# Diagonal score groups of two neighbouring steps in one visit, in a gated attention and maxout kernel

## The chip, the cores and the metric

The kernel runs on one core of one Trainium2 chip, as one program. The metric is the device time of that program in microseconds (us). The time before is the median of three runs; one further execution was recorded by the hardware profiler, and its trace is what the readings below come from.

## The reference

```python
# u, v: (8, 3072, 256)   z: (8, 3072, 64)   moe_w1, moe_w2: (256, 1024)   moe_w_out: (1024, 256)
scores = (1 / S) * z @ z.T                 # per batch, 3072 x 3072, symmetric
attn   = maximum(scores, 0) ** 2
x      = u * (attn @ v)                    # reshaped to 24576 x 256
out    = maximum(x @ w1, x @ w2) @ w_out   # float32
```

`attn` is symmetric: the block (i, j) is the transposed block (j, i).

## The kernel before, in words

A batch has 24 blocks of 128 rows, in six groups of four (`G = 4`). One **step** `n = 6b + s` gives the output rows of group `s` of batch `b`, so there are 48 steps. Its score groups are: the *early* ones (g < s), which an earlier step computed and a DMA transpose turned into a tile `aT`; its *own* ones (g > s), which are computed here; and the diagonal one (g = s). Steps are called s0 to s5 below, by their place in the batch. In batch 0 the steps s0 to s2 take a simpler way and have no diagonal group of this kind (`NDIAG = 2`).

**Scores.** A score tile is a pair of PSUM banks, 128 x 2 x 512 float32 (`psum_pair`, the `mm` pool, three tiles in a ring). An own group takes two tiles (`add_pair`): two matmuls of 512 columns each, which contract over 64 rows and run side by side in the two halves of the array. The diagonal group (`add_diag`) takes one full tile, `(n, None)`, for its upper two row blocks, and one tile half used, `(n, -1)`, for the lower right quarter: two matmuls of 256 columns. Its lower left quarter comes from two small DMA transposes, `("turn", n, None, r)`. ScalarE (ACT) or VectorE (DVE) then reads the PSUM tile with `relu` (L219, L221) into `a_sb` (pool A, 12 tiles in a ring), and `square` works in place (L225, L227). Own groups are turned into `aT` by SyncE's DMA queue (SP), four row blocks in two halves: the first half after its square, the second half after the sum `S1` of the step itself.

**A step on TensorE (PE).** Every product of `attn @ v` goes by a seven-product scheme on sums: three products per job in a first pass (`X` jobs, operands as they are) and four in a second pass (`Y` jobs, on sums `S1` to `S4` that DVE puts into `es`, a ring of four tiles, and `a_sb` or `aT`). A step runs on PE in this order: the last layer `o` of the step three before (40 matmuls), the 12 `X` jobs (six groups, two each), the middle layer `d` of the step two before (16 matmuls into four PSUM tiles of the same `mm` ring, each read by a `g` relu), and the 12 `Y` jobs. The groups come in the order `st.groups`: early, own, diagonal. Both passes use the same two accumulators; between the passes, `e0`, `w` and `t` read them while `d` runs, and after `Y` others do while the next step's `o` runs.

**Visits.** Score matmuls are put between the products in runs of up to three tiles (`WIN = 3`), the *windows* of the code; a run is called a visit here. The list of windows is filled in the order of the steps and of their rows (L972 to L978), so that a batch of 42 tiles has 14 visits. Then they are placed from the last to the first (L1015 to L1020): each goes to the last place that begins no later than its due time and at least `GAP` = 2.4 us before the next visit. Due times (`rows_read`) are 6.5 us before the first `X` job that reads an own row, and 11.5 us for turned rows and for the diagonal. A place must lie at least 0.86 us behind the end of `o` or `d` and 1.7 us ahead of the next one (`free`, L990). In a step of 16.97 us by this plan (4.36 `o`, 3.92 `X`, 3.46 `d`, 5.23 `Y`) that leaves the 4th to 7th `X` jobs, and the `Y` jobs from the third to the ninth. With 2.4 us between visits, a step has at most three: one in `X`, one ahead of the third `Y` job ("early") and one ahead of the ninth ("late").

**The other queues.** PE's order is written out from this plan. A list scheduler then gives every other piece of work an engine and an order: of the work that could begin first, the one with the earliest due time. Each engine, and SP's DMA queue, works in that order and waits in it. `make_zT`'s two transposes (job `zT`) bring the next batch's `z`; from batch 1 on they are let go 12 us into s3. `uT` turns the step's `u`.

Of the kernel before, what the change touches and what calls it, by code (L numbers as in the profile page):

```python
# [11 lines left out]
def kernel(  # L12
# [27 lines left out]
    P = 128  # L40
    NSB = S // P
    G = 4
    WIN = 3
    GW = G * P
    HW = GW // 2
    NG = NSB // G
# [4 lines left out]
    NDIAG = 2  # L51
# [27 lines left out]
    def matmul(*args, **kw):  # L79
        newest[0] = pin(nc.tensor.matmul(*args, **kw)).ins  # L80
# [57 lines left out]
    def direct(b, i, j):  # L138
        return b == 0 and i < j <= NDIR

    q = seqs[0]
# [19 lines left out]
    class Job:  # L161
        def __init__(self, key, ways, fn, deps, new, uses, after, lag):
            self.key, self.ways, self.fn, self.lag = key, ways, fn, lag
            self.deps, self.new, self.uses, self.after = list(deps), new, list(uses), list(after)
            self.succ, self.waits = [], 0
            self.begin = self.done = None
            self.due = 1e12
# [7 lines left out]
    def job(key, ways, fn, deps=(), new=None, uses=(), after=(), lag=100):  # L175
        assert key not in jobs, key
        jobs[key] = Job(key, ways, fn, deps, new, uses, after, lag)

    def buf(pool, key, make):
        bufs[pool, key] = Buf(make)  # L180
        order.setdefault(pool, []).append(key)

    def tile_of(pool, key):
        return bufs[pool, key].tile

    class Step:
        def __init__(self, n, b, s):
            self.n, self.b, self.s, self.q = n, b, s, seqs[b]
            self.plain = n < PLAIN
            self.count = [0] * KD  # L190
            self.last_plain = [None] * KD
            self.diag = not (b == 0 and s <= NDIAG)
            self.rows = ([None] if self.diag else []) + [
                k0
                for k0 in range(0, NSB, 2)
                if k0 // G > s or direct(b, k0 // G, s) or (k0 // G == s and not self.diag)
            ]
            self.early = [i for i in range(s) if not direct(b, i, s)]
            self.own = sorted({k0 // G for k0 in self.rows if k0 is not None})
            self.groups = self.early + self.own + ([s] if self.diag else [])  # L200

    steps = [Step(n, *divmod(n, NG)) for n in range(B * NG)]

    def score(q, out_ps, j, k, s, q0, n):
        half = ds(j * dqk, dqk)
        matmul(
            out_ps,
            q.zT[half, k + 1 - j, :],
            q.zT[half, ds(G * s + 1 - j + q0, n), :],
            start=True,  # L210
            stop=True,
        )

    def turn(out_ap, in_ap):
        sp_dma(out=out_ap, in_=in_ap, transpose=True)

    def relu(eng, out_ap, in_ap):
        if eng == "ACT":
            pin(nc.scalar.activation(out_ap, in_ap, AF.Relu))  # L219
        else:  # L220
            pin(nc.vector.tensor_single_scalar(out=out_ap, in_=in_ap, scalar=0.0, op=ALU.max))  # L221

    def square(eng, ap):
        if eng == "ACT":
            pin(nc.scalar.activation(ap, ap, AF.Square))  # L225
        else:
            pin(nc.vector.tensor_mul(ap, ap, ap))  # L227
# [33 lines left out]
    def a_tile(st, g):  # L261
        return tile_of(*a_key(st.n, g))
# [52 lines left out]
    def s_tile(key):  # L315
        return tile_of("mm", key)
# [61 lines left out]
    def add_diag(st):  # L378
        n, q, g = st.n, st.q, st.s
        k = G * g  # L380
        a = ("A", (n, g))
        buf("A", (n, g), lambda: apool.tile([P, G, GW], bf16, name="a_sb"))

        def low_blocks():
            return a_tile(st, g).rearrange("p r (q x) -> p r q x", x=P)[:, 2:4, 2:4, :]

        def scores(_):
            for j in range(2):
                score(q, s_tile((n, None))[:, j, :], j, k + j, g, 0, G)

        def scores_low(_):
            ps = s_tile((n, -1))
            score(q, ps[:, 0, 2 * P :], 0, k + 2, g, 2, 2)
            score(q, ps[:, 1, : 2 * P], 1, k + 3, g, 2, 2)

        job(("score", n, None), {"PE": 223}, scores, deps=z_deps(st), new=("mm", (n, None)), lag=150)
        job(("score", n, -1), {"PE": 112}, scores_low, deps=z_deps(st), new=("mm", (n, -1)), lag=150)

        def relu_low(eng):
            ps = s_tile((n, -1)).rearrange("p b (q x) -> p (b q) x", x=P)  # L400
            relu(eng, low_blocks(), ps[:, 2:6, :].rearrange("p (r q) x -> p r q x", r=2))

        job(
            ("relu", n, None),
            RELU,
            lambda eng: relu(eng, a_tile(st, g)[:, 0:2, :], s_tile((n, None))),
            deps=[("score", n, None)],
            new=a,
            uses=[("mm", (n, None)), a],
            lag=200,  # L410
        )
        job(
            ("relu", n, -1),
            RELU_HALF,
            relu_low,
            deps=[("score", n, -1)],
            uses=[("mm", (n, -1)), a],
            after=[("relu", n, None)],
            lag=200,
        )  # L420
        job(
            ("square", n, None),
            SQUARE,
            lambda eng: square(eng, a_tile(st, g)[:, 0:2, :]),
            deps=[("relu", n, None)],
            uses=[a],
            lag=200,
        )
        job(
            ("square", n, -1),  # L430
            SQUARE_HALF,
            lambda eng: square(eng, low_blocks()),
            deps=[("relu", n, -1)],
            uses=[a],
            lag=200,
        )
        for r in range(2):

            def do_turn(_, r=r):
                aD = a_tile(st, g).rearrange("p r (q x) -> p r q x", x=P)  # L440
                turn(aD[:, 2:4, r, :], aD[:, r, 2:4, :].rearrange("p q x -> p (q x)"))

            job(
                ("turn", n, None, r),
                {"SP": 450},
                do_turn,
                deps=[("square", n, None)],
                uses=[a],
                lag=2600,
            )  # L450
# [517 lines left out]
    tiles = []  # L968
    for n, st in enumerate(steps):
        for k0 in st.rows:  # L970
            tiles += [(n, None), (n, -1)] if k0 is None else [(n, k0)]
    windows, room = [], 0  # L972
    for i, (n, k0) in enumerate(tiles):
        if not room or (k0 is None and room < 2):
            windows.append([])
            room = 2 if n == 0 else WIN
        windows[-1].append((n, k0))
        room = 0 if (n + 1) % NG == 0 and k0 == -1 else room - 1  # L978

    begins, t = [], 0  # L980
    for ns, _, _, _ in work:
# [18 lines left out]
    for n in range(PLAIN, len(steps)):  # L1000
        i = first_of[n]
# [13 lines left out]
    for w in reversed(range(len(windows))):  # L1015
        limit = min([limit] + [due[r] for r in windows[w] if r in due])
        found = [i for i in spots if begins[i] <= limit]
        i = found[-1] if found else 0
# [29 lines left out]
    def z_deps(st):  # L1048
        return [("zT", st.b)] if st.b else []
# [45 lines left out]
    for n in range(len(steps)):  # L1095
        b, s = steps[n].b, steps[n].s
        if n == 0:
            add_u(0, None)
        else:
            pb, ps = divmod(n - 1, NG)  # L1100
# [15 lines left out]
    for tile_sb, source, key, at, new, rows in (  # L1116
# [16 lines left out]
        deps=[("w2",)],  # L1133
        new=W2T,
        uses=[W2, W2T],
        after=at_step(0, 1, 7),
        lag=3500,
# [5 lines left out]
        deps=[("w1",), ("w2",)],  # L1143
        uses=[W2],
# [3 lines left out]
    def w2o_products(_):  # L1148
# [15 lines left out]
        deps=[("w2T",), ("wo",)],  # L1164
        new=[("mm", ("w2o", dc)) for dc in range(KD)],
        uses=[W2T],
        lag=150,
    )
    for dc in range(KD):
# [4 lines left out]
            deps=[("w2o",)],  # L1174
            uses=[("mm", ("w2o", dc))],
            lag=200,
# [3 lines left out]
    for st in steps:  # L1180
        for k0 in st.rows:
            add_diag(st) if k0 is None else add_pair(st, k0)
    for args in plain_todo:
        st, i, ks, dcs = args
# [58 lines left out]
    for pool, keys in order.items():  # L1243
        for i, k in enumerate(keys):
            j = taker.get((pool, k))
# [21 lines left out]
    for key, before in zip(pe_order, [None] + pe_order):  # L1267
        j = jobs[key]
# [7 lines left out]
    while stack:  # L1276
        j = stack.pop()
# [49 lines left out]
    while len(emitted) < len(jobs) - len(HEAD):  # L1327
        best = None
        for e, todo in ready.items():
            if e == "DVE":  # L1330
                todo = [r for r in todo if not left_to_act(r[1], r[0])]
            if not todo:
                continue
            at, _, j = min(
                ((max(t, idle_from[e]), j.due, j) for t, j in todo), key=lambda x: x[:2]
            )
# [3 lines left out]
        at, e, j = best  # L1340
# [93 lines left out]
```

## Time and profile before

| | |
|---|---|
| median of 3 runs | 932.8 us (932.5 to 934.61) |
| profiled execution, its time | 930.27 us |
| its span, first to last instruction | 928.5 us |
| granted TensorE clock | 1.000 |
| PE / DVE / ACT busy | 923.0 / 766.3 / 682.2 us |
| score matmuls, 512 columns | x594, 64x512 |
| score matmuls, 256 columns | x90, 64x256 |

The span is 1.8 us below that execution's own time, and the execution lies 2.5 us below the median. In the views, `L80` is the one line from which every matmul is issued, so PE's work is told apart by its tiles: `s_ps<-zT` are scores, `acc<-es,...`, `acc<-aT,...` and `acc<-a_sb,...` the products of `X` and `Y`, `s_ps<-xT,w_sb` the layer `d`, `s_ps<-w_out_sb,g_sb` the layer `o`. On ACT, `g_sb<-s_ps` reads a tile of `d`, `a_sb<-s_ps` a score tile.

### The profile page before, as it was taken

To read this page: it belongs to the slowest core of one execution; us is meant where nothing else is said; L and a number is where in the kernel's file an instruction comes from. 1 tells how busy PE (TensorE), PEld (TensorE's weight loads), DVE (VectorE), ACT (ScalarE), POOL (GpSimd) and SP (SyncE) were. 2 spreads that over 40 slices of the span, in tenths; PEclk is the share of its full clock that TensorE was granted. 3 is DMA by queue.
4 is the path that set the end of the run, shared out by engine and by line. 5 is a ranking of instruction groups with operands and counts; after the bars stand their busy time and mean duration, and the time that the engine had idled before them with its cause. 6 is when DMAs were issued, how large, how long until landed. Compare 5 with 4: busy or idle time off the path is not lost.

```text
span 928.5 us, 18994 instructions
## 1 busy us (share of the span) xinstructions
PE 923.0 (99%) x7343; PEld 668.2 (72%) x7343; DVE 766.3 (83%) x1915; ACT 682.2 (73%) x825; POOL 58.4 (6%) x115
## 2 busy tenths in 40 slices
PE   9999999999999999999999999999999999999998
PEld 3367777777777777777777776777767776777786
DVE  7958997888978888888888888888898887988761
ACT  8867876778777777776877678776888658875634
POOL 2100100000000000001000010000000000000000
PEclk9999999999999999999999999999999999999999
DMA  9999999987989879998999899988898888986611
GB/s 161 151 183 180 179 186 181 158 156 136 160 172 157 151 137 180 165 152 144 151 188 153 153 146 158 172 150 153 144 166 173 149 149 149 183 154 125 121 46 68
DMA packets 372778, 142.54 MB, mean 154 GB/s; under 512 B 351184, under 2 KB 352848, under 8 KB 372688
## 3 DMA queue, kind: packets, MB, share of 16 engines
q1 hardware_dynamic: 356128, 111.60, 64.6%
q0 software_dynamic: 16560, 29.74, 22.9%
q8 instruction: 57, 0.93, 0.4%
q14 instruction: 33, 0.27, 0.1%
HBM read 59.77 MB, written 25.17 MB: 91 GB/s over the span
## 4 chain that ended last, share of the span: by engine, by line
PE 94%; DVE 3%; DMA 1%; issue 0%; ACT 0%; POOL 0%; POOLq 0%
PE s_ps L80 47%; PE acc L80 47%; DVE es L233 1%; DMA v_sb<-in_v_dram 1%; DVE a_sb L221 1%; DVE lf L236 0%; DMA o_sb<-in_z_dram 0%; DVE a_sb L233 0%; DVE xT L240 0%; DVE e L233 0%; DVE a_sb L227 0%; DVE g_sb L221 0%; DVE e L236 0%; ACT a_sb L225 0%; ACT a_sb L219 0%
## 5 line engine op out<-in xcount | busy, mean ns | idle before, releaser
L80 PEld LDWEIGHTS <-v_sb 128*128 128x128 bf16 x2304 | 223.7, 98 | 79.9 <-issue 37.7
L219 ACT ACTIVATE a_sb<-s_ps 128x1024 bf16<-128x1024 f32 (+1 forms) x231 | 211.6, 971 | 30.7 <-PE s_ps L80 28.0
L225 ACT ACTIVATE a_sb<-a_sb 128x1024 bf16<-128x1024 bf16 (+1 forms) x220 | 214.2, 1010 | 0.3
L80 PE MATMUL acc<-es,v_sb 128*128 128x256 bf16 x864 | 197.4, 274 | 0.1
L80 PE MATMUL s_ps<-w_out_sb,g_sb 128*128 128x256 bf16 x1504 | 195.0, 273 | 0.0
L219 ACT ACTIVATE g_sb<-s_ps 128x1024 bf16<-128x1024 f32 x181 | 170.9, 1029 | 13.4 <-PE s_ps L80 13.4
L233 DVE TENSOR_TENSOR es<-a_sb 128x512 bf16<-128x512 bf16 x306 | 121.1, 416 | 66.9 <-PE acc L80 66.9
L80 PEld LDWEIGHTS <-lf 128*128 128x128 bf16 x1620 | 158.3, 98 | 22.6 <-issue 0.3
L80 PE MATMUL s_ps<-xT,w_sb 128*128 128x512 bf16 x768 | 173.6, 379 | 0.0
L80 PE MATMUL acc<-es,lf 128*128 128x256 bf16 x756 | 170.8, 273 | 0.0
L80 PE MATMUL acc<-a_sb,lf 128*128 128x256 bf16 x612 | 166.9, 273 | 0.0
L80 PEld LDWEIGHTS <-g_sb 128*128 128x128 bf16 x1504 | 146.9, 98 | 17.5
L80 PE MATMUL acc<-aT,v_sb 128*128 128x256 bf16 x684 | 143.0, 273 | 0.0
L80 PE MATMUL acc<-a_sb,v_sb 128*128 128x256 bf16 (+1 forms) x740 | 138.9, 291 | 0.3 <-ACT a_sb L225 0.3
L80 PEld LDWEIGHTS <-w_sb 128*128 128x128 bf16 x768 | 75.0, 98 | 81.1 <-issue 0.3
L230 ACT COPY e<-acc 128x512 f32<-128x512 f32 x90 | 53.2, 591 | 108.9 <-PE acc L80 108.5
L221 DVE TENSOR_SCALAR a_sb<-s_ps 128x1024 bf16<-128x1024 f32 (+1 forms) x107 | 121.2, 1133 | 5.1 <-PE s_ps L80 4.8
L230 ACT COPY o_sb<-s_ps 128x512 f32<-128x512 f32 (+1 forms) x92 | 53.1, 577 | 86.3 <-PE s_ps L80 86.3
L80 PE MATMUL s_ps<-zT 64*128 64x512 bf16 (+1 forms) x684 | 92.9, 366 | 0.4 <-DVE zT L110 0.4
L227 DVE TENSOR_TENSOR a_sb<-a_sb 128x1024 bf16<-128x1024 bf16 (+1 forms) x118 | 75.0, 647 | 0.2 <-ACT a_sb L219 0.2
L80 PE MATMUL s_ps<-W2o_sb,xT 128*128 128x256 bf16 x384 | 73.4, 273 | 0.0
L80 PE MATMUL acc<-aT,lf 128*128 128x256 bf16 x252 | 68.7, 273 | 0.0
(60 smaller groups left out, 711.8 us busy)
## 6 DMA issues: line engine op xcount, KB each, us to landing
out_dram<-o_sb SPq DMA_DIRECT2D x47, 512.0 KB, 3.7
v_sb<-in_v_dram POOLq DMA_DIRECT2D x48, 256.0 KB, 5.3
u_sb<-in_u_dram POOLq DMA_DIRECT2D x48, 256.0 KB, 5.3
aT<-a_sb SPq DMA_TRANSPOSE x230, 4.2
z_sb<-in_z_dram POOLq DMA_DIRECT2D x7, 384.0 KB, 5.4
a_sb<-a_sb SPq DMA_TRANSPOSE x90, 3.2
w_sb<-in_moe_w_dram POOLq DMA_DIRECT2D x2, 512.0 KB, 9.6
uT<-u_sb SPq DMA_TRANSPOSE x48, 4.6
```

Of the source, the lines that this page charges most:

```text
L80: newest[0] = pin(nc.tensor.matmul(*args, **kw)).ins
L219: pin(nc.scalar.activation(out_ap, in_ap, AF.Relu))
L221: pin(nc.vector.tensor_single_scalar(out=out_ap, in_=in_ap, scalar=0.0, op=ALU.max))
L225: pin(nc.scalar.activation(ap, ap, AF.Square))
L227: pin(nc.vector.tensor_mul(ap, ap, ap))
L230: pin(nc.scalar.copy(out_ap, in_ap) if eng == "ACT" else nc.vector.tensor_copy(out_ap, in_ap))
L233: pin(nc.vector.tensor_add(*args))
```

## The change

Two neighbouring steps with a diagonal group (s0 and s1, s2 and s3, s4 and s5) become a pair; `st.pair` is 0 for the first and 1 for the second. In batch 0 only s4 and s5 are a pair, and s3 stays as it was. The pair's diagonal tiles are computed in one visit of their own: the first's full tile, one tile that holds the lower quarters of both (four matmuls of 256 columns, the first's in the left halves of the two banks, the second's in the right halves), and the second's full tile. Each step keeps its own two relus, squares and small transposes. In the second step of a pair the diagonal group is the first in both passes instead of the last. The visit goes ahead of the first step's own rows in the list of windows, or ahead of the window that is still being filled.

```diff
@@ class Step @@
-            self.groups = self.early + self.own + ([s] if self.diag else [])
+            self.pair = s % 2 if self.diag and not (b == 0 and s - s % 2 <= NDIAG) else None
+            diag = [s] if self.diag else []
+            if self.pair == 1:
+                self.groups = diag + self.early + self.own
+            else:
+                self.groups = self.early + self.own + diag
@@ add_diag @@
+        low = ("mm", (n - (st.pair or 0), -1))
         def scores_low(_):
-            ps = s_tile((n, -1))
-            score(q, ps[:, 0, 2 * P :], 0, k + 2, g, 2, 2)
-            score(q, ps[:, 1, : 2 * P], 1, k + 3, g, 2, 2)
+            ps = tile_of(*low)
+            for i in range(1 if st.pair is None else 2):
+                for j in range(2):
+                    score(q, ps[:, j, ts(i, 2 * P)], j, k + G * i + 2 + j, g + i, 2, 2)
 ...
-        job(("score", n, -1), {"PE": 112}, scores_low, deps=z_deps(st), new=("mm", (n, -1)), lag=150)
+        if st.pair != 1:
+            job(
+                ("score", n, -1),
+                {"PE": 112 if st.pair is None else 223},
+                scores_low,
+                deps=z_deps(st),
+                new=low,
+                lag=150,
+            )
         def relu_low(eng):
-            ps = s_tile((n, -1)).rearrange("p b (q x) -> p (b q) x", x=P)
-            relu(eng, low_blocks(), ps[:, 2:6, :].rearrange("p (r q) x -> p r q x", r=2))
+            ps = tile_of(*low)[:, :, ts(st.pair or 0, 2 * P)]
+            relu(eng, low_blocks(), ps.rearrange("p r (q x) -> p r q x", x=P))
 ...
-            deps=[("score", n, -1)],
-            uses=[("mm", (n, -1)), a],
+            deps=[("score",) + low[1]],
+            uses=[low, a],
@@ the list of windows @@
         for k0 in st.rows:
-            tiles += [(n, None), (n, -1)] if k0 is None else [(n, k0)]
+            if k0 is not None:
+                tiles.append((n, k0))
+            elif st.pair != 1:
+                tiles += [(n, None), (n, -1)] + ([(n + 1, None)] if st.pair == 0 else [])
     windows, room = [], 0
     for i, (n, k0) in enumerate(tiles):
-        if not room or (k0 is None and room < 2):
-            windows.append([])
-            room = 2 if n == 0 else WIN
-        windows[-1].append((n, k0))
-        room = 0 if (n + 1) % NG == 0 and k0 == -1 else room - 1
+        if k0 is None and steps[n].pair == 1:
+            continue
+        if k0 == -1 and steps[n].pair == 0:
+            windows.insert(len(windows) - (room > 0), [(n, None), (n, -1), (n + 1, None)])
+        elif k0 is not None or steps[n].pair is None:
+            if not room or (k0 is None and room < 2):
+                windows.append([])
+                room = 2 if n == 0 else WIN
+            windows[-1].append((n, k0))
+            room -= 1
+        if tiles[i + 1 : i + 2] and tiles[i + 1][0] // NG > n // NG:
+            room = 0
```

## The prediction

> **What bounds the kernel now.** I read the page first: who is busy, and what the chain that ended last is made of.
>
> ```profile
> PE 923.0 (99%) x7343; PEld 668.2 (72%) x7343; DVE 766.3 (83%) x1915; ACT 682.2 (73%) x825; POOL 58.4 (6%) x115
> PE 94%; DVE 3%; DMA 1%; issue 0%; ACT 0%; POOL 0%; POOLq 0%
> ```
>
> PE is busy from end to end. A wait of PE for another engine would stand in the view of waits; the longest two that it lists are these, both of the kernel's first microseconds:
>
> ```profile
> PE zeros L80 <- DVE blank L144: 1.2, 1, 1.2
> PE s_ps L80 <- DVE zT L110: 0.4, 1, 0.4
> ```
>
> So the change is worth what it takes from PE's stream or puts into it. The matmuls stay the same in number and size (two of 256 columns per step before, four per pair after). What changes is where the score runs stand. I therefore read PE's timeline around three visits of batch 3 (start, duration, group):
>
> ```profile
> 314.55 0.27 PE L80 MATMUL acc<-aT,v_sb 128*128 128x256 bf16 x1
> 314.75 0.86 PE L80 MATMUL s_ps<-zT 64*128 64x512 bf16 x6
> 315.54 0.28 PE L80 MATMUL acc<-es,v_sb 128*128 128x256 bf16 x1
> ...
> 318.06 0.27 PE L80 MATMUL acc<-aT,v_sb 128*128 128x256 bf16 x1
> 318.27 0.82 PE L80 MATMUL s_ps<-zT 64*128 64x512 bf16 x6
> 319.02 0.28 PE L80 MATMUL acc<-es,v_sb 128*128 128x256 bf16 x1
> ...
> 337.67 0.27 PE L80 MATMUL acc<-aT,v_sb 128*128 128x256 bf16 x1
> 337.88 0.71 PE L80 MATMUL s_ps<-zT 64*128 64x512 bf16 x6
> 338.52 0.28 PE L80 MATMUL acc<-es,v_sb 128*128 128x256 bf16 x1
> ```
>
> Durations are modelled and overlap, so I take differences of starts: from the last product ahead of the visit to the first behind it. The first is an early visit that holds a diagonal (full, half, full): 0.99. The second is late, three full tiles: 0.96. The third is late, with a diagonal: 0.85. Products follow each other at 0.11, and a tile at 512 columns costs 0.216 (as `d`, 16 matmuls in 3.46). Two and a half tiles are 0.54, three are 0.65. So a visit costs 0.85 - 0.11 - 0.54 or 0.96 - 0.11 - 0.65 = **0.20 us for going in and out**, but the early one with a diagonal costs 0.34. Cutting the window at its third tile shows why (last two matmuls of that visit; below them the same of the early visit of three full tiles that begins at 334.36):
>
> ```profile
> 315.22 0.39 PE L80 MATMUL s_ps<-zT 64*128 64x512 bf16 x2
> ...
> 334.82 0.39 PE L80 MATMUL s_ps<-zT 64*128 64x512 bf16 x2
> ```
>
> The third tile starts 0.47 after the first in both, although the half tile should let it start at 0.33, as in the late visit. It waits for a bank pair: the pool has three, an early visit stands 0.87 us behind the four `d` tiles, and its third tile takes the buffer of the last. ACT's timeline has the end of that:
>
> ```profile
> 312.32 2.85 ACT L219 ACTIVATE g_sb<-s_ps 128x1024 bf16<-128x1024 f32 x3
> 315.19 1.51 ACT L219 ACTIVATE a_sb<-s_ps 128x1024 bf16<-128x1024 f32 x2
> ```
>
> The last `g` relu ends at 315.17, and the tile starts 0.05 later. So an early visit takes 0.99 whatever its second tile is, and the half tile saves nothing there; the view of waits has no row for it.
>
> **The change, part by part.** *How many visits.* A batch has 30 own tiles, 6 full and 6 half ones: 42, or 14 visits. After it, three pair visits of three and 30 own tiles: 39, or 13 visits, all full. In batch 0 only s4 and s5 pair: five tiles in two visits become three and two, still two visits. Seven visits go.
>
> *Where they go.* Walking from the last window to the first with the front part's rules and the plan's times (pairs of rows in order: ten of s0, eight of s1, six of s2, four of s3, two of s4), I get, with s4 and s5 meaning the batch before: s4 early (pair s0/s1), late; s5 in X, early, late; s0 early, late; s1 in X (pair s2/s3), early, late; s2 in X, early (pair s4/s5), late; s3 none. Before it was: s4 early (diagonal), late; s5 in X, early, late (diagonal); s0 in X, early, late (diagonal); s1 early, late; s2 early (diagonal), late; s3 early (diagonal), late (diagonal).
>
> *The sum on PE.* Before: three early ones with a diagonal at 0.99, three late ones with a diagonal at 0.85, two early ones of full tiles at 0.99 (s5, s1), six at 0.96 (the early one of s0 among them, where DVE takes one `g` relu: the by-form groups have 7 of those): 13.26 us. After: four early ones at 0.99, nine at 0.96: 12.60. Each interval holds one product of 0.11 that remains, so 14 x 0.11 and 13 x 0.11 come off: 11.72 and 11.17. That is 0.55 us per batch, of which 0.20 is the visit and the rest half tiles that now are full where the wait had eaten them. Seven batches give 3.85; in batch 0 the late visit of its s3 falls from two and a half tiles to two, 0.11. **Sum: -4.0 us.** Against the profiled execution's 930.27 that is 926.3; against the median, 932.8, it is 928.8, and I forecast the median.
>
> By the Trainium skill (TensorEngine Tiling, Key Properties), a change between whole-array and half-array matmuls drains the array, so a visit pays twice. The same skill (TensorE: Matmul & The Clock Gate, Single matmul latency) puts fill and drain at about 166 ns warm. As an estimate that is 0.33 per visit instead of the 0.20 of the rows, and the sum would be -4.9; the rows decide.
>
> *What I cost at nothing, and its cover.* **Emptying the pair's tiles:** the shared tile is free only after both half relus, the second of which follows the other step's full one. ACT alone needs 1.39 for a full and a half (315.19 to 316.58), 2.78 for all four, from 0.44 after the visit's first matmul: done at 3.22. The next visit wants that buffer at 318.27 - 314.75 + 0.22 = 3.74. In X the second `d` tile wants it 3.6 after the visit starts (visit at 327.21, `d` at 329.94, 0.86 a tile). Cover 0.4 to 0.5, and DVE takes near a third of these relus; without it, each of 22 pair visits (three in seven batches, one in batch 0) would lose the overrun. **Buffers of `a_sb`:** twelve back in the ring, the tightest is the first own tile of s2: it reuses s1's diagonal, whose `Y` jobs are now the first two, directly ahead of that early visit. Last in `Y` they would block it; first, they don't. **The engines:** s1 and s2 get one visit more each. On DVE the own relus and squares take 196 us for 316 tiles, 0.62 a tile, on ACT 431 us, 1.36. A visit adds 1.9 and 4.1 to steps that are thus busy (s0, then s1; after the stretch the sum of it, then busy PE, PEld, DVE, ACT and POOL, clock, DMA share, GB/s):
>
> ```profile
> 340.28:359.74 19.46, 19.46 (x160) 14.16 (x158) 19.46 (x56) 16.66 (x22) 0.53 (x1) 1.00 0.95 174
> 359.74:378.49 18.75, 18.75 (x155) 14.01 (x152) 15.25 (x38) 14.12 (x18) 0.53 (x1) 1.00 0.96 158
> ```
>
> s1 would come to DVE 17.2 and ACT 18.2 of 19.6, close but under; s0, where DVE is full and PE still doesn't wait, loses a visit. **SP's queue:** the small transposes move earlier with their visits. In batch 0 those of s5 are now wanted first in its `X`, at about 97 us; they were issued at 89.8 and landed by 96.3, and their earlier due time puts them one transpose forward.
>
> **The rivals.** *The late turn (slower).* In s3 the own group 4 becomes the fifth in order instead of the fourth, so its sums need a fifth `es` buffer: `S1` waits until the first group's `Y` jobs are done, and the second half of its turn with it. It used to be issued well ahead of `zT`; now `zT` is let go first. SP's queue there, in batch 2:
>
> ```profile
> 290.49 1.24 SPq L83 DMA_TRANSPOSE aT<-a_sb  x1
> 293.89 1.23 SPq L83 DMA_TRANSPOSE uT<-u_sb  x1
> 295.21 5.83 SPq L83 DMA_TRANSPOSE zT<-z_sb  x2
> 301.13 2.48 SPq L83 DMA_TRANSPOSE a_sb<-a_sb  x2
> ```
>
> The turn moves from 290.49 to about 301.1, 5.5 us after s3's second `Y` job (295.6). s4's `X` jobs read it as fourth group, which without visits in s3 is 11 x 0.44 + 4.36 + 6 x 0.33 = 11.1 after that job. That leaves it 5.6 to land, where the page's median for `aT` is 4.2. It costs PE only the excess, in six batches (not in 0, which keeps its order in s3, nor in the last, which has no `zT`). It decides from 6.6 on: 1.0 x 6 takes the gain and 2 us more. At the 6 to 7 us that landings take a little later in s4, when `v` loads run, it is up to 1.6 x 6 = 9.6, so 938.4. For it: DMA is at 0.95 in these stretches. Against it: SP is free there at 4.2 to 5.5 in the six batches, and transposes issued there landed within 2.3 to 4.
>
> *Only the visits go.* If the early visits lose as much elsewhere (a later `g` relu, because ACT has the X visits of s1 and s2 to empty first), 7 x 0.20 = 1.4 stay: 931.4, no difference that can be told.
>
> *The pair visit is emptied too slowly.* The Trainium skill warns (TensorEngine Tiling, PSUM Bottleneck) that side-by-side matmuls don't speed up the emptying of PSUM. By rows: if square or sums get ahead of one half relu by 1 us, each pair visit loses 0.5 to 0.6 on `d` or on the next visit, 22 x 0.55 = 12 us less the 4.0: 940.9. Against it is that today relus follow each other on ACT directly behind a visit, with squares after them.
>
> **How the numbers follow.** Forecast, -3.2 to -4.9: 0.64. Only the visits, or small losses of the other kinds: 0.17. Late turn: 0.12; slow emptying or a full engine in s1: 0.07. 0.2% is 1.9 us, about what can be told from no change. Faster 0.65, same 0.17, slower 0.18. The forecast's own range is 927.9 to 929.6 about 928.8. To leave out no more than 2 in 10 it goes up through the second case and the start of the slower ones, to 933.5, and down to 927.4 for a median that is drawn low.
>
> **What would show it.** Right: score runs 109 instead of 116; every early visit at 0.99; none in s3; no new row of PE waiting. Wrong: PE waiting for a DMA `aT<-a_sb` or with idle ahead of s4's fourth group (late turn); more than 0.20 between in and out at late or X visits, or `d` longer than 3.46 behind the X visit of s1 (emptying); DVE or ACT without a gap in s1 and s2 and PE idle ahead of `Y`.

## The result, and the profile after

Timed against each other in 20 runs each, the changed kernel takes 928.12 us in the median and the kernel before 932.65: a ratio of 0.9960, 95% interval 0.9949 to 0.9971. On 932.65 that is -3.7 us, between -4.8 and -2.7; the medians themselves lie 4.5 apart. The profiled execution took 926.03 us with a span of 924.3.

The page after, busy time and the chain that ended last:

```profile
PE 918.9 (99%) x7343; PEld 669.9 (72%) x7343; DVE 787.4 (85%) x1956; ACT 656.3 (71%) x784; POOL 58.4 (6%) x115
PE 99%; DMA 0%; ACT 0%; DVE 0%; issue 0%
```

PE has the same 7343 matmuls and is still busy throughout; its busy time and the span fell together, by 4.1 and 4.2 us. DVE took 41 pieces of work more and ACT 41 fewer. The view of waits after has PE waiting in the same four places as before, all in the first 9 us; the two that the prediction showed are now:

```profile
PE zeros L80 <- DVE blank L144: 1.2, 1, 1.2
PE s_ps L80 <- DVE zT L110: 0.3, 1, 0.3
```

For a reading that batch 0 doesn't blur I take the time between the same point of two batches: the first matmul of layer `o` in s4 of batches 2 and 3. In PE's timeline of the kernel before:

```profile
302.04 0.27 PE L80 MATMUL s_ps<-w_out_sb,g_sb 128*128 128x256 bf16 x1
...
415.88 0.27 PE L80 MATMUL s_ps<-w_out_sb,g_sb 128*128 128x256 bf16 x1
```

That is 113.84 us for six steps. In PE's timeline of the changed kernel the same two matmuls, and two pair visits with the products around them:

```profile
277.38 0.27 PE L80 MATMUL acc<-aT,v_sb 128*128 128x256 bf16 x1
277.59 0.82 PE L80 MATMUL s_ps<-zT 64*128 64x512 bf16 x8
278.34 0.28 PE L80 MATMUL acc<-es,v_sb 128*128 128x256 bf16 x1
...
300.57 0.27 PE L80 MATMUL s_ps<-w_out_sb,g_sb 128*128 128x256 bf16 x1
...
313.08 0.27 PE L80 MATMUL acc<-aT,v_sb 128*128 128x256 bf16 x1
313.29 0.92 PE L80 MATMUL s_ps<-zT 64*128 64x512 bf16 x8
314.14 0.28 PE L80 MATMUL acc<-es,v_sb 128*128 128x256 bf16 x1
...
413.86 0.27 PE L80 MATMUL s_ps<-w_out_sb,g_sb 128*128 128x256 bf16 x1
```

Six steps now take 113.29, which is **0.55 less**, in every batch from the second to the seventh. The pair visits are the runs of x8: four matmuls of 512 columns and four of 256. The early one of s2 takes 0.96 from product to product, the early one of s4 1.05 (differences are taken before the views round to hundredths). There are 109 score runs where there were 116, and none in s3 from batch 1 on.

### The profile page after: what moved, and what is told of

The parts are those of the page before. It is cut to its first block, busy times and chain, and to the rows that moved or that the text cites. A ratio compares the mean times of both kernels' runs of the same rounds, so it can differ in the third digit from the quotient of the medians.

```text
span 924.3 us, 19018 instructions
## 1 busy us (share of the span) xinstructions
PE 918.9 (99%) x7343; PEld 669.9 (72%) x7343; DVE 787.4 (85%) x1956; ACT 656.3 (71%) x784; POOL 58.4 (6%) x115
## 4 chain that ended last, share of the span: by engine, by line
PE 99%; DMA 0%; ACT 0%; DVE 0%; issue 0%
PE s_ps L80 50%; PE acc L80 49%; DMA o_sb<-in_z_dram 0%; ACT a_sb L231 0%; ACT a_sb L225 0%; PE tpz L109 0%; DVE zT L110 0%; ACT o_sb L236 0%; DVE z_sb L154 0%
## 5 line engine op out<-in xcount | busy, mean ns | idle before, releaser
L225 ACT ACTIVATE a_sb<-s_ps 128x1024 bf16<-128x1024 f32 x211 | 204.1, 1021 | 41.0 <-PE s_ps L80 37.9
L231 ACT ACTIVATE a_sb<-a_sb 128x1024 bf16<-128x1024 bf16 (+1 forms) x215 | 207.0, 1011 | 0.2
L225 ACT ACTIVATE g_sb<-s_ps 128x1024 bf16<-128x1024 f32 x173 | 163.5, 1028 | 10.8 <-PE s_ps L80 10.8
L80 PE MATMUL acc<-a_sb,v_sb 128*128 128x256 bf16 (+1 forms) x740 | 142.3, 291 | 0.3 <-ACT a_sb L231 0.3
L227 DVE TENSOR_SCALAR a_sb<-s_ps 128x1024 bf16<-128x1024 f32 (+1 forms) x127 | 129.4, 1034 | 0.7 <-PE s_ps L80 0.7
L236 ACT COPY o_sb<-s_ps 128x512 f32<-128x512 f32 (+1 forms) x84 | 48.3, 575 | 93.8 <-PE s_ps L80 93.6
L80 PE MATMUL s_ps<-zT 64*128 64x512 bf16 (+1 forms) x684 | 89.1, 366 | 0.3 <-DVE zT L110 0.3
L233 DVE TENSOR_TENSOR a_sb<-a_sb 128x1024 bf16<-128x1024 bf16 (+1 forms) x123 | 78.8, 651 | 0.2 <-ACT a_sb L225 0.2
```

The source lines that it names most:

```text
L236: pin(nc.scalar.copy(out_ap, in_ap) if eng == "ACT" else nc.vector.tensor_copy(out_ap, in_ap))
```

## The experiments

All whole-run ratios below are against the kernel before, timed beside it on the same chip, with their 95% intervals. "Six steps" is the reading above, taken in each run's own trace; in one kernel it repeats within 0.01 us from batch to batch where nothing is said.

**1. Only the order.** The kernel before, with the groups in the new order and nothing else:

```diff
-            self.groups = self.early + self.own + ([s] if self.diag else [])
+            diag = [s] if self.diag else []
+            second = s % 2 == 1 and self.diag and not (b == 0 and s - 1 <= NDIAG)
+            self.groups = diag + self.early + self.own if second else self.early + self.own + diag
```

> The kernel before, with the diagonal group first in the second step of each pair and nothing else: 116 visits, no shared tile. Theory A (the gain is what leaves PE's stream: 0.20 us for each visit that goes, and the wait of an early visit's third tile for the last g relu, which eats a half tile): with the new due times the plan moves one diagonal visit per batch from the early place of s2 into X, where its half tile counts (0.99 to 0.85), so 7 x 0.14 = -1.0 us against before, about 931.6, ratio 0.999. Theory B (the gain is from the order: diagonal buffers free earlier, turns earlier, DVE and ACT loaded otherwise): most of the change's -4 us, ratio 0.996.

Measured: ratio 0.9993 (0.9976 to 1.0011), six steps 113.75, 0.09 less than before. The diagonal visit that moved into X fell to 0.85 as expected (-0.14); the early diagonal visit of s3 rose to 1.05 (+0.06). So the order is worth 0.1 per batch, and that by a visit that it moves; theory B is out as the main cause.

**2. The early place one job later, kernel before.**

```diff
-        return all(end <= at - 860 or at + 1700 <= beg for beg, end in shared)
+        return all(end <= at - 1290 or at + 1700 <= beg for beg, end in shared)
-    GAP_FIRST, GAP = 2100, 2400
+    GAP_FIRST, GAP = 2100, 2100
```

> The kernel before, with the early place one Y job later (0.44 us, 1.29 instead of 0.86 behind d; the late visit stays, so the gap falls to 2.18): same 116 visits, same tiles and order, only the distance to the last g relu grows. Theory A: the third tile no longer waits; three early visits with a diagonal fall from 0.99 to 0.85 and two full ones from 0.99 to 0.96 per batch, 0.50 x 7 = 3.5, and 0.2 in batch 0: -3.7 us against before, ratio 0.996. Theory B, or any other cause of the 0.14: no change, ratio 1.000.

Measured: ratio 1.0065 (1.0039 to 1.0090), slower. The timeline has both halves of the answer: an early diagonal visit of this kernel, and a `Y` product of the same step's end.

```profile
302.98 0.27 PE L80 MATMUL acc<-aT,v_sb 128*128 128x256 bf16 x1
303.19 0.71 PE L80 MATMUL s_ps<-zT 64*128 64x512 bf16 x6
303.84 0.28 PE L80 MATMUL acc<-es,v_sb 128*128 128x256 bf16 x1
...
308.22 0.27 PE L80 MATMUL acc<-es,v_sb 128*128 128x256 bf16 x1 [0.40 <-DVE es L233]
```

The visit takes 0.85 now: the wait for the `g` relu is gone, and all visits of a batch together are 0.49 shorter. But the last sums of s2 and s3 come late: PE waits for DVE ahead of the diagonal's `Y` jobs, two waits per batch that add 0.45 and 0.56, and a short one in s1 adds 0.13. Six steps take 114.49, which is 113.84 with these four terms. The sign of the forecast was wrong because with the visits DVE's order changed too. In DVE's timeline a relu of the late visit now stands directly ahead of the last sum that PE waits for:

```profile
306.62 1.22 DVE L221 TENSOR_SCALAR a_sb<-s_ps 128x1024 bf16<-128x1024 f32 x1
307.75 0.42 DVE L233 TENSOR_TENSOR es<-a_sb,es 128x512 bf16<-128x512 bf16 x1
```

In the kernel before, at the same place, that sum begins at 300.16, ahead of the late visit's relu (300.50), and is done 0.6 us before its product begins. In s2 the order changed in the same way.

**3. The same, changed kernel** (the same two lines):

> The changed kernel with the early place one Y job later. Theory A: its early visits (1.05 in s4, 0.96 in s5, 0.99 in s0 and s1, 0.96 in s2) all come to 0.96, 0.17 x 7 + 0.1 = -1.3 us against the changed kernel, so about -5.4 against before, ratio 0.994; the difference to the second kernel of this call is then the seven visits alone, 1.4 to 1.7 us. Theory B: nothing on top of the change's own -4, ratio 0.996.

Measured: ratio 0.9951 (0.9930 to 0.9973); six steps 113.13, 0.16 less than the changed kernel, as expected, and every early visit at 0.96. (The expectation swaps two visits of the changed kernel: s5's takes 0.99 and s1's 0.96; their sum is the same.) Here s3 has no visit any more and its last group is an own one, and no late sum shows in the steady batches. In batch 0, whose s3 keeps the old order, PE waited twice for a late sum, 2.55 and 0.77 us, and the whole-run gain over the changed kernel isn't resolved.

**4. The pair visit cut in two.** The second step's full tile is put behind the next product job:

```diff
+        held_back = []
 ...
+                if steps[n].pair == 1 and k0 is None:
+                    held_back.append((n, k0))
-                if ("score", n, k0) not in HEAD:
+                elif ("score", n, k0) not in HEAD:
 ...
         pe_order.append(key)
+        for n, k0 in held_back:
+            pe_order.append(("score", n, k0))
```

> The changed kernel with each pair visit cut in two: first and shared tile, then one X or Y job, then the second's full tile. Same tiles, same order of groups, 22 more visits. Theory A: 22 x 0.20 = 4.5, less 0.1 x 8 because the tile that waited in an early pair visit now comes later: +3.7 us against the changed kernel, about -0.3 against before, ratio 1.000. Theory B: the order and the shared tile are still there, so -3 to -4 stays, ratio 0.996 to 0.997.

Measured: ratio 0.9994 (0.9976 to 1.0012); six steps 113.84, 0.55 above the changed kernel, the whole gain. The small new visit in PE's timeline of this kernel:

```profile
317.49 0.27 PE L80 MATMUL acc<-aT,v_sb 128*128 128x256 bf16 x1
317.70 0.39 PE L80 MATMUL s_ps<-zT 64*128 64x512 bf16 x2
318.02 0.28 PE L80 MATMUL acc<-es,v_sb 128*128 128x256 bf16 x1
```

From product to product it is 0.53: one product's 0.11, one tile's 0.22, and 0.20 for going in and out. Three more visits per batch at 0.20 are 0.61, less 0.06 to 0.1 for the wait that the tile no longer meets. That the kernel comes out level with the one before is a coincidence of sizes: it has two visits more than that one (0.40), and no half tile lost ahead of a wait (0.32). The new order, which it keeps, is not what the gain hangs on.

**5 and 9. The half tile last.** The kernel before, with the half tile as third of its visit:

```diff
-            tiles_w = sorted(windows[w], key=lambda r: r[1] not in (None, -1))
+            tiles_w = sorted(windows[w], key=lambda r: 0 if r[1] is None else 2 if r[1] == -1 else 1)
```

> The kernel before, with the half tile as the third instead of the second of its visit, nothing else. Theory A (the third tile of an early visit waits for the buffer that the last g relu frees, 0.47 after the first tile): two full tiles cover 0.43 of that, and the half tile behind the wait costs 0.11 instead of 0.22, so the three early diagonal visits per batch fall from 0.99 to 0.88; late ones stay at 0.85. Six steps take 0.32 less (113.84 to 113.52 between the same points of two batches), 7 x 0.32 + 0.1 = -2.3 us, ratio 0.9975. Rival (the 0.14 hangs on the half tile itself, or on ACT's order): no change, 113.84.

The timed runs gave 0.9945 (0.9925 to 0.9965), better than expected. The trace of the fifth can't be set beside the others (1922.78 us), so the ninth is the same kernel again, for its trace:

> The fifth kernel again, unchanged, for a profile (the fifth's execution under the profiler ran at half speed and tells nothing of its waits; its timed runs came out at a ratio of 0.9945, below the 0.9975 that was expected). Theory A as sized before: early diagonal visits at 0.88, 113.52 per six steps, ratio 0.9975. Rival (something besides the early visits gets shorter when the half tile is last): under 113.4 per six steps, or a shorter batch 0, ratio 0.995.

Measured the second time: ratio 0.9961 (0.9943 to 0.9979); six steps 113.52, to the hundredth as expected. The early diagonal visit of s4 in its timeline takes 0.88:

```profile
318.64 0.27 PE L80 MATMUL acc<-aT,v_sb 128*128 128x256 bf16 x1
318.84 0.75 PE L80 MATMUL s_ps<-zT 64*128 64x512 bf16 x6
319.52 0.28 PE L80 MATMUL acc<-es,v_sb 128*128 128x256 bf16 x1
```

The third tile starts 0.46 us after the first, as it did when the half tile was second (0.47). So the 0.14 is the third tile's wait, and which tile is behind the wait decides what it costs. Both whole-run ratios lie below the 0.9975 that the steady batches explain, the second with an interval that holds it; what else got shorter, if anything, stays open.

**6. The turn of s3 later still.** In the changed kernel, that turn behind three more transposes, and `uT` of s4 later:

```diff
-                after=() if first else [("turn", n, k0 - 2)],
+                after=() if first else [("turn", n, k0 - 2)] + (
+                    [("turn", n, k0 + 4), ("turn", n + 1, k0 + 2), ("uT", n + 1)]
+                    if st.s == 3 and 0 < st.b < B - 1 and k0 == G * g + 2 and g == 4
+                    else []
+                ),
 ...
-            after=at_step(*divmod(n - 1, NG), 9) if n else (),
+            after=at_step(*divmod(n - 1, NG), 12.3 if s == 4 and 0 < b < B - 1 else 9) if n else (),
```

> The changed kernel, with the second half of the turn of s3's group 4 sent behind three more transposes on SP's queue (uT of s4, the second half for group 5, the first half of s4's group 5) in batches 1 to 6. In the changed kernel it lands 2.25, 2.53, 3.63, 3.63, 1.68 and 1.71 us ahead of s4's fourth group. Late-turn mechanism: issued some 3.8 us later, it lands behind that point in all six, and PE waits there by the excess: 1.6 + 1.3 + 0.2 + 0.2 + 2.1 + 2.1 = 7.5 us, more if it then meets the v loads (landings of 6 to 7): +7 to +19 against the changed kernel, ratio against before 1.003 to 1.016. If turns are hidden anyway: no change, 0.996.

Measured: ratio 0.9984 (0.9965 to 1.0002). SP got through the others faster than I had reckoned, so the turn was issued only 0.2 to 2.8 us later, and landed between 1.65 ahead of s4's fourth group and 0.18 behind it. PE has no wait there; DVE, which reads the turned tile for a sum, waited for it in two batches, 0.56 and 1.01 us. PE has one in three of the six batches, at another place; PE's timeline in batch 2:

```profile
318.62 0.27 PE L80 MATMUL acc<-es,lf 128*128 128x256 bf16 x1 [0.84 <-DVE t L239]
```

and the line of DVE's timeline ahead of it, a fold (a sum of rows of `v` that the products read):

```profile
316.88 0.29 DVE L242 TENSOR_TENSOR lf<-v_sb 128x256 bf16<-128x256 bf16 x1 [3.82 <-DMA v_sb<-in_v_dram]
```

DVE stands for 3.82 us before the fold, for a `v` load; `w` and `t`, which free an accumulator for `Y`, are queued behind it. The load is no later than in the changed kernel: POOL issues it 4.83 us into s4 in all six batches of both kernels, and it lands 10.1 to 11.2 us into s4 here, 10.3 to 11.3 there. What differs is DVE's order. In the changed kernel the same fold stands behind `t`, and PE loses nothing to it:

```profile
309.96 0.41 DVE L239 TENSOR_TENSOR t<-e,acc 128x256 f32<-128x256 f32 x1
...
311.37 0.29 DVE L242 TENSOR_TENSOR lf<-v_sb 128x256 bf16<-128x256 bf16 x1 [0.54 <-DMA v_sb<-in_v_dram]
```

Six steps take 114.20, 113.78 and 113.74 in these three batches and 113.29 in the other three. So the edit cost 1.85 us in these batches, instead of the 7 to 19 that were expected, and by the order that the scheduler gave DVE with it. What a late turn costs PE is not shown. In batch 0 PE waited 2.2 us for an `aT` and 2.6 for a small transpose; experiment 10, which is the changed kernel itself, has 1.7 at the first spot and experiment 1 has 2.4 at the second, so these aren't put down to the edit.

**7 and 8. Own groups ahead of early ones** in the second step, without and with the later early place:

```diff
-                self.groups = diag + self.early + self.own
+                self.groups = diag + self.own + self.early
```

> The changed kernel, with the second step's groups in the order diagonal, own, early instead of diagonal, early, own: S1 of s3's group 4 needs no fifth es buffer, and its turn goes ahead of zT again. Late-turn mechanism as I read it (a margin that is small but positive costs nothing): the margin ahead of s4's fourth group grows from 1.7 to 3.6 to some 10 us, PE's stream stays, 113.29 per six steps within 0.1, ratio 0.996. Rival (the shrunk margin already costs): below 113.2 and a ratio of 0.995 or less.

> The seventh kernel with the early place one Y job later as in the third. Theory A: early visits all at 0.96, 113.13 per six steps as in the third kernel, 1.2 us below the changed kernel, ratio 0.9945 to 0.995. Rival (as in the second kernel, the later place makes the last sums late): PE waits for DVE in Y, over 113.3, ratio 0.997 or more.

Measured: the seventh 0.9951 (0.9932 to 0.9971), six steps 113.37; the turn lands 9.4 to 11.7 us ahead. The margin grew as expected and the time didn't fall (0.08 more, nearly all of it in the early visit of s1, 1.03 instead of 0.96). The eighth: 0.9953 (0.9936 to 0.9971), six steps 113.13 from batch 1 on.

**10 and 11. The changed kernel beside its variant.** The eleventh was meant to be the third with the later place from s4 of batch 0 on only:

```diff
-        return all(end <= at - 1290 or at + 1700 <= beg for beg, end in shared)
+        lead = 1290 if at >= starts[LAG + 1] else 860
+        return all(end <= at - lead or at + 1700 <= beg for beg, end in shared)
```

> The changed kernel again, as the base of the next one on the same chip: 113.29 per six steps, ratio 0.996.

> The changed kernel with the early place one Y job later from s4 of batch 0 on, but not in batch 0's s3, whose diagonal is still last and where the third kernel lost 1.0 us to a late sum. Theory A: 113.13 per six steps, no wait of 1 us in batch 0's s3: 1.1 to 1.3 us below the tenth kernel, ratio about 0.9947. Rival (the later place costs as much elsewhere): the tenth's ratio.

Measured: 0.9941 (0.9919 to 0.9964) and 0.9946 (0.9923 to 0.9968), medians 928.11 and 928.23. Six steps are 113.29 and 113.13. But the edit of the eleventh doesn't do what it was meant to: in batch 0's s3 the early visit stands 13.16 us behind the start of `o`, as in the third, where the changed kernel has 12.72. A visit goes to the last place that is allowed, and the smaller `GAP` alone allows the later one. So the eleventh is the third over again, with work in the same order on PE, DVE and SP: it waits twice for late sums in batch 0's s3, 0.56 and 0.77 us, and loses 0.5 in batch 1, and its forecast was not tested. A better version than the changed kernel is not shown.

The steady readings side by side, six steps each:

| kernel | visits | six steps, us | against before |
|---|---|---|---|
| before | 14 | 113.84 | |
| 1, order only | 14 | 113.75 | -0.09 |
| 9, half tile last | 14 | 113.52 | -0.32 |
| 2, before, early place later | 14 | 114.49 | +0.65 |
| changed | 13 | 113.29 | -0.55 |
| 4, pair visit in two | 16 | 113.84 | 0.00 |
| 7, own first | 13 | 113.37 | -0.47 |
| 3, 8, 11, early place later | 13 | 113.13 | -0.71 |

## Why the prediction was right, point by point

**The sum on PE** held: 0.55 us per batch was forecast and 0.55 is what the traces show. Seven batches of it and the 0.1 of batch 0, whose s3 is 0.11 shorter, are 4.0, inside the measured -4.8 to -2.7. The two traces differ by 4.2; what goes beyond the sum lies in batches 0 and 1, where, to name the largest, the changed kernel came 0.26 later to s3 and the kernel before lost 0.42 once. The sum is made of the two parts that were named. The 0.20 for a visit is what experiment 4 pays back three times per batch. The half tile that an early visit wasted is what experiment 9 regains in another way, 0.32 per batch. The two make 0.52, and the rest is in the single visits.

**Single visits** were off by a few hundredths that cancel, and that is luck: of the five early ones only s5's came as forecast. The one of s4 takes 1.05 instead of 0.99, those of s1 and s2 0.96 instead of 0.99, and s0's 0.99 instead of 0.96. The wait for the last `g` relu is there where I had it, in ACT's timeline of the changed kernel:

```profile
310.91 2.85 ACT L225 ACTIVATE g_sb<-s_ps 128x1024 bf16<-128x1024 f32 x3
313.72 1.94 ACT L225 ACTIVATE a_sb<-s_ps 128x1024 bf16<-128x1024 f32 x2
```

The last relu ends at 313.76, and the pair visit of 313.29 goes on with its third tile at 313.81. But which engine takes which `g` relu is the scheduler's affair and changed with the load: DVE took 7 of them before and takes 15 now. In s1 and s2 it takes the first of the four, ACT is done earlier, and the early visits, at 0.96, have no such wait.

**Emptying the pair's tiles** cost nothing, as forecast. At the visit of 313.29 the scheduler gave the two half relus to DVE beside ACT's two full ones. They are done at 315.66, 2.4 us after the visit began, where ACT alone had been put at 3.2, and the late visit behind it is at 0.96. By the Trainium skill (TensorEngine Tiling, PSUM Bottleneck) both engines should empty PSUM; here both do, and the cover is larger for it.

**The late turn** came as its mechanism said, and its price was nought. SP's queue of the changed kernel at that place:

```profile
293.52 1.43 SPq L83 DMA_TRANSPOSE uT<-u_sb  x1
295.04 5.96 SPq L83 DMA_TRANSPOSE zT<-z_sb  x2
301.09 4.02 SPq L83 DMA_TRANSPOSE aT<-a_sb  x3
```

The turn is issued at 301.09, where 301.1 was forecast. In the six batches it landed 3.3 to 5.0 after its issue, 1.7 to 3.6 ahead of s4's fourth group; in the kernel before it landed some 13 ahead. Experiment 7 shows that a larger margin is worth nothing as long as the small one is above zero. That a margin below zero would be paid in X, at the group that reads it, is not shown: experiment 6 brought it to between 1.65 and -0.18, and what PE lost there in s4 came from DVE's order.

**The engines** came near their limit as forecast, but the other one. The stretches of s0 and s1 (sum, then busy PE, PEld, DVE, ACT, POOL; the last columns are not used):

```profile
338.98:357.72 18.74, 18.74 (x154) 14.06 (x152) 18.20 (x54) 13.51 (x18) 0.53 (x1) 1.00 1.11 194
357.72:377.29 19.57, 19.57 (x162) 14.26 (x160) 18.96 (x45) 15.29 (x20) 0.53 (x1) 1.00 0.69 121
```

s1 comes to DVE 18.96 and ACT 15.29 of 19.57, where 17.2 and 18.2 were forecast: I had shared the new visit's work out by the averages of before, and the scheduler gave more of it to DVE. s0, full before, has 0.5 us of air.

**By the Trainium skill** (TensorEngine Tiling, Key Properties), a change of the array's mode drains it. As an estimate, its figure for the fixed part of a single matmul's latency (TensorE: Matmul & The Clock Gate, Single matmul latency: about 166 ns), paid twice per visit, would have made the sum -4.9. The small visit of experiment 4 shows 0.20 for the two changes, so the rows' price was the right one.

## What to carry to other kernels

Where one engine is busy throughout, differences of start times around a recurring pattern show its price better than busy times do: here 0.20 us for going into half-array matmuls and back, and 0.14 us that no list of waits named. A smaller piece of work saves only if it stands behind the wait, not ahead of it; the half tile did nothing as second tile and something as third. Moving a visit can change another engine's order, and one job's distance was enough to make DVE's last sums late; in experiment 6 the new order cost more than the late transfer that was to be tested.

## What the runs showed that was not expected

Steady batches repeat to 0.01 us, while batch 0 does not: layer `o` in step 6 (s0 of batch 1) begins at 112.2 us in the profile of before, at 112.4 in that of the change, and between 113.1 and 117.5 in those of experiments 6 to 11. Single runs of one kernel scatter by 6 us (926.03 to 932.41 for the changed one), more than the change itself is worth, so effects of half a microsecond per batch were told apart by the traces and not by the times.
